# Pads, token-block sums on VectorE, an evened-out token loop and a wider slot for the query divisions in a gated attention and expert kernel

## The chip, the cores and the metric

The kernel runs on one core of one Trainium2 chip, as one launch. The metric is the device time of that launch in microseconds (us); the median of three runs of the kernel before is 2440.28 us, and they lie between 2435.78 and 2441.69 us. TensorE is called PE in the profile, its weight loads PEld, VectorE is DVE, ScalarE is ACT, GpSimd is POOL and SyncE is SP. The profile comes from one more execution of its own.

## The reference

For 2048 tokens of width 512 the result is `g*a + (1-g)*b`, all in float32:

```python
g = sigmoid((x * gate_w).sum(-1))                 # one gate per token
# a: linear attention, 32 heads of width 16
q, k, v = split(x @ wqkv);  pq, pk = phi(q), phi(k)   # phi(t) = (t+1 if t>0 else exp(t)) + 1e-6
kv = sum over tokens of pk * v;  z = sum over tokens of pk
a  = ((pq @ kv) / (pq . z + 1e-6)) @ wo
# b: 8 experts, all of them used (K = E = 8), weighted by a softmax of x @ w_gate
b  = sum over e of gates[e] * (silu(x @ w1[e]) @ w2[e])   # w1: 512x1792, w2: 1792x512
```

## The kernel before

**Numbers.** A float32 operand is split into a high part that TensorE's `float32r` form holds and the rest: ScalarE copies the high part (`act_copy`, L63), VectorE subtracts it (`split`, L267). A product then is three matmuls (`mm3`, L58 to L60: high by high, high by low, low by high).

**Seven products.** The two large products of each expert are computed on 2x2 blocks with seven block products in place of eight. So the kernel needs sums and differences of blocks of x, of the weights and of the hidden values. `prep(g, step)` makes the operands of weight group g in eight steps and writes the blocks of w2 to DRAM (`w2stash`); `x_sum` and `x_part` make those of x.

**The key stage, `keys` (L249 to L497).** It loops over 16 tiles of 128 tokens, t = 0 to 15. `load_x` brings x transposed, 512 tokens at a time; `split_x(tb, k)` splits a quarter of such a block. `g_proj(t, g)` computes keys and gate logits of a tile in two groups of columns (256 and 266); `g_done` applies phi: two ScalarE passes and one VectorE pass per group, then a high copy on ScalarE and a low pass on VectorE into the tile `pkh`, and a POOL DMA that adds the tile's keys to the key sum `pks` (L395). `load_xt` brings x untransposed and `split_xt(t)` splits it into the tile `xt`. `y_acc(t)` then adds x^T pk of the tile to four PSUM banks, 12 matmuls; it is called one tile late. Each engine takes its instructions in the order in which the program lists them, so a ScalarE copy that waits holds all that ScalarE has behind it.

Beside the tiles, at hand-set values of t, stand `x_sum` (four sums of blocks of 1024 columns for each half of the tokens; ScalarE negates the target and a POOL DMA adds the other block to it), `x_part` (splits a sum; for the second half of the tokens two SP DMAs of 512 KB store it in `xstash`), `x_keep` (stores three blocks that were split as they are) and, from t = 12, two steps of `prep(0, .)` per tile.

**The expert stage, `experts` (L501 on).** It steps through ticks u = 0, 1, 2, ... Seven ticks make a weight group. A tick's `up` does one of the seven products of the hidden layer (6 matmuls, banks a, b, c); from u = 44 on each tick also does a slice of the second product (`tick`, 6 matmuls into p, weights from the tiles `w2`). `high` and `low_h` split the hidden values into `ho`, `differ` forms their sums. Between ticks of the start stand `state` (kv of the attention, 16 float32 matmuls, u = 1), `fold` (u = 3 to 6), `gates` (u = 5), `normaliser` (u = 8), `gate_rows` (u = 10), the opening of the pool of the w2 tiles (u = 12) and `load_wb` (u = 14). Query columns pass the same way as a ninth expert, whose phi is stored to DRAM by SP (L553, 16 DMAs of 256 KB); just then `x_next` loads the second half's blocks of x back from `xstash`, on SP too.

**The divisions.** After that, in the ticks of the first four experts of the second half, `queries_first` and `queries_last` divide 512 tokens' queries by their normaliser, in slots s = 0 to 11 of 98 ticks each: s = 0 to 3 form the denominator, s = 4 to 6 invert it in four VectorE reciprocals (L860), multiply and split it, and the matmuls n (L879) spread it over the columns in slots s = 7 to 10, each followed by a VectorE multiply (L867) one slot later. The matmuls n share the two buffers of bank a with the up products.

Of the kernel before, what the change touches and what calls it, by code (L numbers as in the profile page):

```python
# [10 lines left out]
F32 = mybir.dt.float32  # L11
F32R = mybir.dt.float32r
# [25 lines left out]
def f32(ap):  # L38
    return ap.bitcast(F32)
# [3 lines left out]
def gated_mix_kernel(ctx: ExitStack, tc: tile.TileContext, xT, x, wk, wv, wqkv_q, wo, wm, out):  # L43
# [73 lines left out]
    misc = ExitStack()  # L117
    m.misc = misc.enter_context(tc.tile_pool(name="misc", bufs=1, side="right"))
    weights(m)
    keys(m)  # L120
# [128 lines left out]
def keys(m):  # L249
# [87 lines left out]
    def load_xt(tb):  # L337
        r = m.raw_tile(f"xr{tb}") if tb < 3 else room(f"xr{tb}")
        xr[tb] = r.rearrange("p (t d) -> p t d", d=D)
        nc.sync.dma_start(xr[tb], m.x[tb * TB:(tb + 1) * TB, :].rearrange("(t p) d -> p t d", p=P))  # L340
# [72 lines left out]
    def x_sum(p, step):  # L413
        a, b = raw[2 * p], raw[2 * p + 1]
        b11, b21, b12, b22 = a[:, :2], a[:, 2:], b[:, :2], b[:, 2:]
        dst, src = ((b11, b12), (b12, b22), (b22, b11), (b21, b22))[step]
        if step < 3:
            act_copy(dst, dst, scale=-1.0)
        nc.gpsimd.dma_start(dst, src, accum_op=ALU.add)

    def x_part(p, i):
# [8 lines left out]
        if i == 3:  # L430
            act_copy(h, r, scale=-1.0)
            v.scalar_tensor_tensor(lo, r, -1.0, f32(h), op0=ALU.mult, op1=ALU.subtract)
        else:
            split(r, h, lo)
        if p:
# [21 lines left out]
    ys = [dn_bank(f"y{i}") for i in range(KT)]  # L457
    x_sum(0, 0)
    for t in range(NTT - 1):
        y_acc(t)  # L460
        split_x(1, t)
    split_x(1, KT - 1)
    for t in range(NTT, NT):
        tb, tt = divmod(t, NTT)
        if t in (4, 8, 11):
            load_xt((t + 1) // 4)
        if t in (4, 5):
            load_x(t - 2)
        if t in (11, 12):
            m.load(t - 11)  # L470
        for g in range(2):
            g_proj(t, g)
        split_xt(t)
        if tb == 1:
            split_x(2, tt)
        if t in (8, 9):
            split_x(3, 2 * t - 16), split_x(3, 2 * t - 15)
        y_acc(t - 1)
        for p, at in ((0, t), (1, t - 6)):
            if at in (4, 6, 7):  # L480
                x_sum(p, at // 2 - 1 if at < 7 else 3)
            if at in (4, 6, 8, 9):
                x_part(p, {4: 1, 6: 5, 8: 3, 9: 6}[at])
        if t == 8:
            x_sum(1, 0)
        if t == 11:
            x_keep(0, (2, 0)), x_keep(2, (2, 1)), x_keep(4, (3, 1))
        if t > 11:
            m.prep(0, 2 * t - 24), m.prep(0, 2 * t - 23)
    y_acc(NT - 1)  # L490
# [10 lines left out]
def experts(m, misc):  # L501
# [42 lines left out]
    def hidden(g, f, t, dst, src):  # L544
        part, q = groups[g]
        if part.e < E:
            nc.scalar.activation(dst, src, AF.Silu)  # L547
            raw[g, f, t] = dst
            return
        if dst is src:  # L550
            dst = r_tile(f"e{g}_{f}{t}")
        phi(dst, src)
        nc.sync.dma_start(m.pqd[part.h, t, 2 * q + f], dst)  # L553

# [289 lines left out]
    def queries_first(i, s):  # L844
# [4 lines left out]
        elif s == 4:  # L849
# [6 lines left out]
            nc.gpsimd.memset(f32(Q.un[2 * NH:, 0]), 0.0)  # L856
        if s in (4, 5, 6):
            for at in ((0,), (1, 2), (3,))[s - 4]:
                r = Q.r[:, at * P:(at + 1) * P]
                v.reciprocal(r, r)  # L860
        if s == 6:
            v.tensor_mul(Q.r, Q.r, Q.gate)
            act_copy(Q.un[:NH, 0], Q.r)
            v.tensor_sub(Q.un[NH:2 * NH, 0], Q.r, f32(Q.un[:NH, 0]))
        if 8 <= s < 8 + KT:
            d = Q.d[:, s - 8]
            v.scalar_tensor_tensor(d, d, EPS, Q.ps, op0=ALU.add, op1=ALU.mult)  # L867
            nc.sync.dma_start(m.pqd[h, j, s - 8], d)

    def queries_last(i, s):  # L870
        if 0 <= s < KT:
            if s == 0:
                Q.ps = ps_tile(f"dn{i}", "a")
            for j in range(2):
                nc.tensor.matmul(Q.ps[:2 * NH, :], Q.z[:, s], Q.un[:, j], start=(s == 0 and j == 0),
                                 stop=(s == KT - 1 and j == 1))
        elif 7 <= s < 7 + KT:
            Q.ps = ps_tile(f"n{i}_{s}", "a")
            nc.tensor.matmul(Q.ps, Q.spread[:, s - 7], Q.un[:, 0], start=True, stop=True)  # L879

# [39 lines left out]
    for u in range(LAG1 + NTICK):  # L920
# [5 lines left out]
        s -= 3  # L926
        query = u >= U1 and 0 <= i < 4 and s < 12

# [128 lines left out]
```

## Time and profile before

| what | value |
|---|---|
| median of three runs | 2440.28 us |
| time of the profiled execution | 2439.3 us |
| its span | 2437.3 us |
| granted TensorE clock, mean | 0.993 |
| PE busy | 2386.7 us, 98% |
| PEld busy | 1940.2 us, 80% |
| DVE busy | 1821.5 us, 75% |
| ACT busy | 1419.3 us, 58% |
| DMA bytes | 516.52 MB |

The table's busy times are sums over stages with different limits. Matmuls overlap, so their mean duration is longer than the distance from one to the next. A row of a timeline gives start, duration, engine, line, operation, tiles and count, and in square brackets how long the engine sat idle before it and what ended that. A row of waits reads: who, on whom, us in total, times, longest. A row of a table by stretches gives the stretch, its length, then the busy time and the count of each engine, the granted clock, the DMA engines' busy share and GB/s.

### The profile page before, as it was taken

To read this page: it belongs to the slowest core of one execution; us is meant where nothing else is said; L and a number is where in the kernel's file an instruction comes from. 1 tells how busy PE (TensorE), PEld (TensorE's weight loads), DVE (VectorE), ACT (ScalarE), POOL (GpSimd) and SP (SyncE) were. 2 spreads that over 40 slices of the span, in tenths; PEclk is the share of its full clock that TensorE was granted. 3 is DMA by queue.
4 is the path that set the end of the run, shared out by engine and by line. 5 is a ranking of instruction groups with operands and counts; after the bars stand their busy time and mean duration, and the time that the engine had idled before them with its cause. 6 is when DMAs were issued, how large, how long until landed. Compare 5 with 4: busy or idle time off the path is not lost. (4 is left out here: it accounts for less than half of the span.)

```text
span 2437.3 us, 31414 instructions
## 1 busy us (share of the span) xinstructions
PE 2386.7 (98%) x10483; PEld 1940.2 (80%) x10483; DVE 1821.5 (75%) x3099; ACT 1419.3 (58%) x2656; POOL 150.6 (6%) x208
## 2 busy tenths in 40 slices
PE   8899999999999999999999999999999999999998
PEld 7777888888888888888778787878878888888876
DVE  5578878888888888888776767777676666666678
ACT  5566666666666666566655555555555555555454
POOL 2110000000000000000000000000000000000021
PEclk9999999999999999999999999999999999999999
DMA  7988888988888888988864444454544444454477
GB/s 203 252 279 287 254 280 248 271 257 265 263 260 279 251 269 253 283 256 261 284 229 117 148 138 165 140 161 148 159 156 139 138 139 146 140 145 138 135 268 271
DMA packets 298706, 516.52 MB, mean 212 GB/s; under 512 B 24352, under 2 KB 192176, under 8 KB 298160
## 3 DMA queue, kind: packets, MB, share of 16 engines
q1 hardware_dynamic: 275840, 468.03, 57.4%
q0 software_dynamic: 22704, 46.49, 10.2%
q8 instruction: 82, 1.34, 0.2%
q14 instruction: 80, 0.66, 0.1%
HBM read 344.61 MB, written 161.42 MB: 208 GB/s over the span
## 5 line engine op out<-in xcount | busy, mean ns | idle before, releaser
L58 PE MATMUL p<-ho,w 128*128 128x512 f32 x1624 | 645.6, 398 | 2.7 <-ACT p L63 1.9
L60 PE MATMUL p<-ho,w 128*128 128x512 f32 x1624 | 645.3, 397 | 0.0
L59 PE MATMUL p<-ho,w 128*128 128x512 f32 x1624 | 638.9, 393 | 0.0
L671 DVE TENSOR_TENSOR ho<-s,ho 128x512 fp32r<-128x512 f32 x784 | 536.1, 685 | 55.2 <-ACT ho L63 53.5
L63 ACT ACTIVATE ho<-s 128x512 fp32r<-128x512 f32 x784 | 486.4, 621 | 18.8 <-PE p L60 11.7
L58 PEld LDWEIGHTS p<-ho,w 128*128 128x128 f32 x1624 | 305.1, 188 | 76.1 <-ACT p L63 6.6
L60 PEld LDWEIGHTS p<-ho,w 128*128 128x128 f32 x1624 | 304.9, 188 | 74.3
L59 PEld LDWEIGHTS p<-ho,w 128*128 128x128 f32 x1624 | 305.5, 188 | 71.6
L547 ACT ACTIVATE s<-s 128x512 f32<-128x512 f32 x224 | 141.8, 633 | 280.5 <-DVE s L609 200.2
L609 DVE TENSOR_TENSOR s<-c,s 128x512 f32<-128x512 f32 x116 | 80.2, 692 | 160.3 <-PE c L60 150.7
L63 ACT ACTIVATE o<-rm 128x512 fp32r<-128x512 f32 x240 | 136.7, 570 | 82.2 <-PE a L60 63.1
L63 ACT ACTIVATE o<-rs 128x512 fp32r<-128x512 f32 x224 | 127.3, 568 | 63.7 <-PE a L60 60.1
L63 ACT ACTIVATE ws<-rm 128x512 fp32r<-128x512 f32 (+1 forms) x217 | 121.8, 571 | 59.2 <-DMA w2stash<-ws 52.5
L615 DVE TENSOR_TENSOR s<-a,s 128x512 f32<-128x512 f32 x116 | 79.9, 689 | 80.0 <-PE a L60 79.9
L547 ACT ACTIVATE s<-b 128x512 f32<-128x512 f32 x112 | 67.3, 601 | 114.2 <-PE b L60 108.9
L63 ACT ACTIVATE s<-a 128x512 f32<-128x512 f32 x116 | 69.4, 598 | 103.9 <-PE a L60 103.9
L183 DVE TENSOR_TENSOR o<-rs,o 128x512 fp32r<-128x512 f32 x168 | 114.8, 683 | 13.8 <-ACT o L63 13.0
L183 DVE TENSOR_TENSOR o<-rm,o 128x512 fp32r<-128x512 f32 x180 | 123.1, 684 | 1.5 <-ACT o L63 1.4
L201 DVE TENSOR_TENSOR ws<-rm,ws 128x512 fp32r<-128x512 f32 x164 | 112.3, 684 | 4.8 <-ACT ws L63 4.8
L63 ACT ACTIVATE s<-c 128x512 f32<-128x512 f32 x116 | 69.0, 595 | 33.4 <-PE c L60 33.3
L63 ACT ACTIVATE b<-a 128x512 f32<-128x512 f32 x116 | 67.1, 578 | 25.0 <-PE a L60 24.9
L705 POOL DMA_DIRECT2D acct<-c x28 | 23.9, 855 | 931.6 <-DVE c L701 702.2
(289 smaller groups left out, 4534.1 us busy)
## 6 DMA issues: line engine op xcount, KB each, us to landing
w<-w2stash SPq DMA_DIRECT2D x406, 512.0 KB, 3.9
w2stash<-ws SPq DMA_DIRECT2D x381, 256.0 KB, 4.3
rm<-wm SPq DMA_DIRECT2D x224, 256.0 KB, 5.3
rs<-wm SPq DMA_DIRECT2D x112, 256.0 KB, 3.7
wb<-wgtd SPq DMA_DIRECT2D x16, 512.0 KB, 5.1
acct<-c POOLq DMA_DIRECT2D x28, 256.0 KB, 6.3
acct<-d POOLq DMA_DIRECT2D x28, 256.0 KB, 5.4
acct<-k POOLq DMA_DIRECT2D x28, 256.0 KB, 5.7
```

The lines of the kernel that those rows point to most:

```text
L58: nc.tensor.matmul(ps, wh, xh, start=start, stop=False, skip_group_check=True)
L59: nc.tensor.matmul(ps, wh, xl, start=False, stop=False, skip_group_check=True)
L60: nc.tensor.matmul(ps, wlo, xh, start=False, stop=stop, skip_group_check=True)
L63: nc.scalar.activation(dst, src, AF.Copy, scale=scale, bias=bias)
L183: v.tensor_sub(two(o, 1), src, f32(two(o, 0)))
L201: v.tensor_sub(two(w, 1), src, f32(two(w, 0)))
L547: nc.scalar.activation(dst, src, AF.Silu)
L609: v.tensor_add(sn[g, 2], bank[g, "c"], sn[g, 2])
L615: v.tensor_add(sn[g, 3], bank[g, "a"], sn[g, 3])
L671: v.tensor_sub(h[:, 1], s, f32(h[:, 0]))
L705: nc.gpsimd.dma_start(m.acct[part.h, j, dt], s, accum_op=ALU.add)
```

## The change

It has five parts.

1. **Pads.** A tile of 96 bytes a partition is allotted first in the pool `misc` and first in the pool of the w2 tiles, and set to zero by GpSimd. `gat` and `mx` get 128 bytes instead of 64, and the projection weights g1 get 8576 bytes instead of 8512, so all that the pool `att` holds behind them lies 64 bytes higher.
2. **Sums on VectorE.** `x_sum` becomes one VectorE subtraction of 1024 columns; the ScalarE negations and the accumulating POOL DMAs go. The sign of one block changes with it, so `x_part` loses its special case.
3. **The token loop.** A table `beside` sets the work of each tile: two or four pieces a tile from t = 4 to 13, all of `prep(0, .)` at t = 14 and 15. `split_xt` of rows 14 and 15 moves to tiles 12 and 13. Loads move ahead, except the two weight loads, which move from t = 11, 12 to t = 12, 14; the three `x_keep` pairs move from t = 11 to t = 6, 9 and 10.
4. **The start of the expert stage.** `state` and what follows it come four to six ticks later.
5. **Queries.** Slots go from 12 to 20: one reciprocal a slot from s = 5 to 8, multiply at 9, split at 10, the matmuls n at 14 to 17. The 16 stores of the queries go from the SP queue to the POOL queue.

```diff
@@ gated_mix_kernel
+    def pad(pool):
+        nc.gpsimd.memset(pool.tile([P, 24], F32, name="pad", tag="pad", bufs=1), 0.0)
+    m.pad = pad
+    pad(m.misc)
@@ keys
-    m.gat = misc.tile([P, NT], F32, name="gat")
-    m.mx = misc.tile([P, NT], F32, name="mx")
+    m.gat = misc.tile([P, 2 * NT], F32, name="gat")[:, :NT]
+    m.mx = misc.tile([P, 2 * NT], F32, name="mx")[:, :NT]
...
-    gw = [att.tile([P, 2 * KT * G[i]], F32R, name=f"g{i}").rearrange("p (c k f) -> p c k f", c=2, k=KT) for i in range(2)]
+    gw = [att.tile([P, 2048 + 96 * i], F32R, name=f"g{i}")[:, :2 * KT * G[i]] for i in range(2)]
...
-        r = m.raw_tile(f"xr{tb}") if tb < 3 else room(f"xr{tb}")
+        xr[tb] = m.raw_tile(f"xr{tb}").rearrange("p (t d) -> p t d", d=D)
@@ x_sum
-        dst, src = ((b11, b12), (b12, b22), (b22, b11), (b21, b22))[step]
-        if step < 3:
-            act_copy(dst, dst, scale=-1.0)
-        nc.gpsimd.dma_start(dst, src, accum_op=ALU.add)
+        dst, x, y = ((b11, b12, b11), (b12, b22, b12), (b22, b22, b11), (b21, b21, b22))[step]
+        v.tensor_sub(dst, x, y)
@@ the loop over tiles
-    x_sum(0, 0)
+    load_xt(1)
+    load_x(2)
     for t in range(NTT - 1):
         y_acc(t)
         split_x(1, t)
     split_x(1, KT - 1)
+    beside = {t: [] for t in range(NTT, NT)}
+    for k in range(KT):
+        beside[4 + k // 2].append(lambda k=k: split_x(2, k))
+        beside[8 + k // 2].append(lambda k=k: split_x(3, k))
+        beside[(4, 5, 6, 6)[k]].append(lambda k=k: x_sum(0, k))
+        beside[(7, 7, 8, 9)[k]].append(lambda k=k: x_part(0, (1, 5, 3, 6)[k]))
+        beside[(10, 10, 12, 12)[k]].append(lambda k=k: x_sum(1, k))
+        beside[(11, 11, 13, 13)[k]].append(lambda k=k: x_part(1, (1, 5, 3, 6)[k]))
+        beside[14].append(lambda k=k: m.prep(0, k))
+        beside[15].append(lambda k=k: m.prep(0, 4 + k))
+    rows_of = {12: (12, 13), 13: (14, 15), 14: (), 15: ()}
     for t in range(NTT, NT):
-        if t in (4, 8, 11):
-            load_xt((t + 1) // 4)
-        if t in (4, 5):
-            load_x(t - 2)
-        if t in (11, 12):
-            m.load(t - 11)
+        if t in (4, 8):
+            load_xt(t // 4 + 1)
+        if t == 5:
+            load_x(3)
+        if t in (12, 14):
+            m.load(t // 2 - 6)
         for g in range(2):
             g_proj(t, g)
-        split_xt(t)
-        if tb == 1:
-            split_x(2, tt)
-        if t in (8, 9):
-            split_x(3, 2 * t - 16), split_x(3, 2 * t - 15)
+        for row in rows_of.get(t, (t,)):
+            split_xt(row)
         y_acc(t - 1)
-        for p, at in ((0, t), (1, t - 6)):
-            if at in (4, 6, 7):
-                x_sum(p, at // 2 - 1 if at < 7 else 3)
-            if at in (4, 6, 8, 9):
-                x_part(p, {4: 1, 6: 5, 8: 3, 9: 6}[at])
-        if t == 8:
-            x_sum(1, 0)
-        if t == 11:
-            x_keep(0, (2, 0)), x_keep(2, (2, 1)), x_keep(4, (3, 1))
-        if t > 11:
-            m.prep(0, 2 * t - 24), m.prep(0, 2 * t - 23)
+        for do in beside[t]:
+            do()
+        if t in (6, 9, 10):
+            i, key = {6: (0, (2, 0)), 9: (2, (2, 1)), 10: (4, (3, 1))}[t]
+            x_keep(i, key)
@@ hidden
-        nc.sync.dma_start(m.pqd[part.h, t, 2 * q + f], dst)
+        nc.gpsimd.dma_start(m.pqd[part.h, t, 2 * q + f], dst)
@@ queries_first
-        if s in (4, 5, 6):
-            for at in ((0,), (1, 2), (3,))[s - 4]:
-                r = Q.r[:, at * P:(at + 1) * P]
-                v.reciprocal(r, r)
-        if s == 6:
+        if 5 <= s < 9:
+            r = Q.r[:, (s - 5) * P:(s - 4) * P]
+            v.reciprocal(r, r)
+        elif s == 9:
             v.tensor_mul(Q.r, Q.r, Q.gate)
+        elif s == 10:
             act_copy(Q.un[:NH, 0], Q.r)
             v.tensor_sub(Q.un[NH:2 * NH, 0], Q.r, f32(Q.un[:NH, 0]))
-        if 8 <= s < 8 + KT:
+        if 15 <= s < 15 + KT:
@@ queries_last
-        elif 7 <= s < 7 + KT:
+        elif 14 <= s < 14 + KT:
@@ the loop over ticks
-        query = u >= U1 and 0 <= i < 4 and s < 12
+        query = u >= U1 and 0 <= i < 4 and s < 20
...
-        if u == 1:
+        if u == 5:
             state()
-        if u in (3, 4, 5, 6):
-            fold(u - 3)
-        if u == 5:
+        if u in (7, 8, 9, 10):
+            fold(u - 7)
+        if u == 11:
             gates()
-        if u == 8:
+        if u == 13:
             normaliser()
-        if u == 10:
+        if u == 15:
             gate_rows()
-        if u == 12:
+        if u == 17:
             misc.close()
             m.w2p = ctx.enter_context(tc.tile_pool(name="w2p", bufs=1, side="right", reuse_waits="tile"))
-        if u == 14:
+            m.pad(m.w2p)
+        if u == 20:
             load_wb(0)
```

More of the change, by code (lines that the diff above doesn't have):

```diff
@@ L314, in split_x @@
         split(raw[tb][:, k, :], xk(0, tb, k), xk(1, tb, k))
-    gw = [att.tile([P, 2 * KT * G[i]], F32R, name=f"g{i}").rearrange("p (c k f) -> p c k f", c=2, k=KT) for i in range(2)]
+    gw = [att.tile([P, 2048 + 96 * i], F32R, name=f"g{i}")[:, :2 * KT * G[i]] for i in range(2)]
+    gw = [g.rearrange("p (c k f) -> p c k f", c=2, k=KT) for g in gw]
     g0, g1 = gw
@@ L337, in load_xt @@
     def load_xt(tb):
-        r = m.raw_tile(f"xr{tb}") if tb < 3 else room(f"xr{tb}")
-        xr[tb] = r.rearrange("p (t d) -> p t d", d=D)
+        xr[tb] = m.raw_tile(f"xr{tb}").rearrange("p (t d) -> p t d", d=D)
         nc.sync.dma_start(xr[tb], m.x[tb * TB:(tb + 1) * TB, :].rearrange("(t p) d -> p t d", p=P))
@@ L428, in x_part @@
             h, lo = both[:, 0], both[:, 1]
[L430 to L434, printed above, removed]
+        split(r, h, lo)
         if p:
@@ L856, in queries_first @@
             nc.gpsimd.memset(f32(Q.un[2 * NH:, 0]), 0.0)
-        if s in (4, 5, 6):
-            for at in ((0,), (1, 2), (3,))[s - 4]:
-                r = Q.r[:, at * P:(at + 1) * P]
-                v.reciprocal(r, r)
-        if s == 6:
+        if 5 <= s < 9:
+            r = Q.r[:, (s - 5) * P:(s - 4) * P]
+            v.reciprocal(r, r)
+        elif s == 9:
             v.tensor_mul(Q.r, Q.r, Q.gate)
+        elif s == 10:
             act_copy(Q.un[:NH, 0], Q.r)
             v.tensor_sub(Q.un[NH:2 * NH, 0], Q.r, f32(Q.un[:NH, 0]))
-        if 8 <= s < 8 + KT:
-            d = Q.d[:, s - 8]
+        if 15 <= s < 15 + KT:
+            d = Q.d[:, s - 15]
             v.scalar_tensor_tensor(d, d, EPS, Q.ps, op0=ALU.add, op1=ALU.mult)
-            nc.sync.dma_start(m.pqd[h, j, s - 8], d)
+            nc.sync.dma_start(m.pqd[h, j, s - 15], d)
     def queries_last(i, s):
@@ L876, in queries_last @@
                                  stop=(s == KT - 1 and j == 1))
-        elif 7 <= s < 7 + KT:
+        elif 14 <= s < 14 + KT:
             Q.ps = ps_tile(f"n{i}_{s}", "a")
-            nc.tensor.matmul(Q.ps, Q.spread[:, s - 7], Q.un[:, 0], start=True, stop=True)
+            nc.tensor.matmul(Q.ps, Q.spread[:, s - 14], Q.un[:, 0], start=True, stop=True)
     def load_query(h, i):
```

1 line of the change is left out of this document (removed).

## The prediction

> **What bounds the kernel now.** I read the page first, then the busy times by stretch, then PE's waits, then the rows around each wait.
>
> ```profile
> span 2437.3 us, 31414 instructions
> PE 2386.7 (98%) x10483; PEld 1940.2 (80%) x10483; DVE 1821.5 (75%) x3099; ACT 1419.3 (58%) x2656; POOL 150.6 (6%) x208
> ```
>
> ```profile
> 30.80:123.80 93.00, 77.36 (x445) 68.12 (x444) 48.65 (x91) 50.62 (x104) 20.55 (x25) 0.91 0.83 215
> 123.80:149.00 25.20, 19.47 (x85) 14.84 (x83) 10.83 (x24) 12.46 (x22) 0.00 (x0) 0.93 0.70 228
> 149.00:190.00 41.00, 41.00 (x186) 33.98 (x187) 38.91 (x67) 33.13 (x67) 8.45 (x17) 1.00 0.98 317
> 205.00:1170.00 965.00, 965.00 (x4187) 785.77 (x4186) 805.42 (x1332) 611.89 (x1154) 40.98 (x48) 1.00 0.86 265
> ```
>
> PE is the bound: from 205 to 1170 us it never pauses, and the change leaves its matmuls as they are. It can gain only where PE stands still or runs at a lower clock, some 50 us in all (2437.3 less 2386.7). The token tiles 4 to 15 (30.8 to 123.8 us) are the worst place: 77.4 busy of 93, with a clock of 0.91, while no other engine is over 51 of 93. So the tiles there wait in turn for something, and these rows say for what:
>
> ```profile
> PE y L58 <- ACT xt L63: 15.6, 3, 6.4
> PE kv L777 <- DMA wv<-wv: 3.9, 2, 2.9
> PE a L58 <- DVE s L615: 2.1, 2, 1.8
> ```
>
> ```profile
> ACT xt L63 <- DMA xstash<-x20h: 8.5, 1, 8.5
> ACT x L63 <- DMA x<-x: 7.2, 1, 7.2
> ACT t L63 <- DMA xstash<-t: 4.5, 1, 4.5
> ```
>
> Three times y waits for the ScalarE copy of xt, 15.6 us together. Each time ScalarE itself stood before a DMA: behind tile 4 before the accumulating POOL DMA of a sum, at tile 12 before the store of x20 that frees the xt tile of row 12, behind tile 14 before the store of a split sum.
>
> **Part 1, the token tiles.** The start of the pkh copy dates each tile; the last row is PE's touch after the last y:
>
> ```profile
> 35.05 0.63 ACT L63 ACTIVATE pkh<-pk 128x512 fp32r<-128x512 f32 x1 [0.49 <-DVE pk L74]
> 57.76 0.63 ACT L63 ACTIVATE pkh<-pk 128x512 fp32r<-128x512 f32 x1 [0.49 <-DVE pk L74]
> 85.98 0.63 ACT L63 ACTIVATE pkh<-pk 128x512 fp32r<-128x512 f32 x1 [0.49 <-DVE pk L74]
> 117.30 0.63 ACT L63 ACTIVATE pkh<-pk 128x512 fp32r<-128x512 f32 x1 [0.49 <-DVE pk L74]
> ...
> 118.51 0.80 PE L58 MATMUL y<-pkh,xt 128*128 128x512 f32 x1 [6.37 <-ACT xt L63]
> 123.82 0.54 PE L559 MATMUL b<-x00h,o 128*128 128x512 f32 x1
> ```
>
> Tiles 7 to 12 (57.76 to 85.98) ran undisturbed: 28.2 us for five, 5.64 each, PE never idle. Tiles 4 to 15 took 82.25 us for eleven; at 5.64 they take 62.0, so 20.2 us go if all three waits go. The last y took 5.3 us (118.51 to 123.82) at the lowered clock after its wait; y is half of a tile's columns (12 matmuls of 512 against 24 of 256 or 266), 2.8 of the 5.64: another 2.5.
>
> Do they go? The DMA accumulation is replaced by VectorE, which needs no copy before it. The x20 store is issued at tile 6, six tiles ahead of its use, the other two pairs at 9 and 10. The store of a split sum now has two tiles (11 us) instead of less. The price of a tile on VectorE, with these durations:
>
> ```profile
> L74 DVE SCALAR_TENSOR_TENSOR pk<-pk,g 128x256 f32<-128x256 f32 x24 | 9.8, 419 | 10.5 <-ACT g L73 10.5
> L80 DVE SCALAR_TENSOR_TENSOR pkh<-pk,pkh 128x512 fp32r<-128x512 f32 x12 | 8.3, 693 | 8.4 <-ACT pkh L63 8.4
> L267 DVE TENSOR_TENSOR xt<-xr,xt 128x512 fp32r<-128x512 f32 x12 | 8.2, 684 | 8.4 <-ACT xt L63 8.4
> L267 DVE TENSOR_TENSOR t<-x,t 128x1024 fp32r<-128x1024 f32 x3 | 3.7, 1229 | 2.3 <-ACT t L63 2.3
> L391 DVE COPY lg<-g 128x10 f32<-128x10 f32 x12 | 1.9, 162 | 0.0
> L63 ACT ACTIVATE x<-x 128x1024 f32<-128x1024 f32 x5 | 5.2, 1046 | 7.2 <-DMA x<-x 7.2
> ```
>
> Base: 2 x 0.42 + 0.69 + 0.16 + 0.68 = 2.37, and 0.70 of wait for the pkh copy (8.4 over 12) = 3.07. A sum of 1024 columns, not shown before, I price at the split of the same size, 1.23 (bounds: 0, if it fits an idle spot, and 1.23). Tiles 4, 5, 8, 9: two splits and one such pass, 3.07 + 1.37 + 1.23 = 5.67. Tiles 6, 7, 10, 11: two such passes, 5.53. Tiles 12, 13 have a second xt: 6.2. Tiles 14, 15 without xt, with four steps of prep each (three to six passes of 0.68, some of half width): about 6.0 and 6.5. Over 5.64 that is 4 x 0.03 + 2 x 0.57 + 0.36 + 0.9 = 2.5; I charge 3 (bounds 0 and 14, second rival). ScalarE loses six passes of 1.05 and stays under VectorE. Eight accumulations leave the POOL queue, so the key sums behind them come sooner. The earlier loads stand on SP before anything that waits: `load_xt(2)` and `(3)` need rows already split. The weight loads come later, behind the stores of tiles 11 and 13 on SP; what needs the first is prep two tiles (11 us) on. **Sum: 20.2 + 2.5 - 3 = -19.7, I take -20** (range 0 to -23).
>
> **Part 2, the start of the expert stage.** PE waits 3.9 us for wv because kv stands one tick after the drain; four ticks later the up products cover the load. With the 2.1 us for VectorE's s and the clock of 0.93 over 25.2 us (half clock for 3.5 us, 1.7 us of work), up to 7.7 us can go. But prep of group 0, its seven stores of w2 blocks, two pairs of xstash stores, the load of group 1, wv, wo and the load of group 2 now fall into some 25 us, and 149 to 190 us shows what full DMA engines move: 317 GB/s at a share of 0.98. I take -3, nearer the full cover of wv alone (bounds -7.7 and +8, first rival). `fold`, `gates`, `normaliser`, `gate_rows` (17 POOL DMAs), the w2 pool and `load_wb` move by five ticks, and the first w2 load is due only at u = 39, so I cost them at nothing; were that cover gone, p would wait for w2 by the same five ticks.
>
> **Part 3, the divisions.** All 16 matmuls n, and the reciprocals:
>
> ```profile
> L879 PE MATMUL n<-az 128*128 128x512 f32 x16 | 7.0, 439 | 6.6 <-DVE pq L867 3.7 <-DVE az L864 2.9
> ...
> L860 DVE RECIPROCAL r<-r 32x128 f32<-32x128 f32 x16 | 14.5, 922 | 0.1
> ```
>
> PE loses 6.6 us: 2.9 because the split of the inverse comes as n is due, 3.7 because the second n waits for the bank, whose reader on VectorE is behind after four reciprocals (3.7 us). With the split at s = 10 and n at 14, the first goes; at s = 15 the backlog is long worked off, though two `differ` passes a tick stand there instead of one. **-6** (bounds -6.6 and +2, four such waits of half a microsecond).
>
> **Part 4, the query stores on POOL.** They wait for phi, and on SP they hold the loads of x behind them:
>
> ```profile
> PE c L58 <- DMA n4h<-xstash: 2.6, 1, 2.6
> ...
> SPq L553 <- DVE e L74: 9.2, 4, 3.3
> ```
>
> ```profile
> 1210.00:1220.00 10.00, 9.35 (x41) 7.25 (x39) 8.29 (x16) 6.85 (x14) 1.71 (x2) 1.00 1.05 377
> ```
>
> But the DMA engines are full then (share 1.05), so an earlier issue mostly lengthens the queue. POOL has nothing urgent: its accumulations wait for VectorE anyway. I take 0 (bounds -3 and +1).
>
> **Part 5, the pads.** What matters is which tiles move. The pool on the right ends at a fixed place, and in the built program its tiles ascend from its base in the order of allotment: the pad lies below the w2 tiles, which keep their addresses (217056, 221152 and 225248, 32 past a multiple of 64). Only `att` shifts, to multiples of 128. So p's weights stay where they are; the two small memsets are nothing. I take 0 (bounds -1 and +1, 384 g and 192 y matmuls at a few ns).
>
> **Sum against the profiled execution: 2439.3 - 20 - 3 - 6 = 2410 us.** That execution stands 1 us below the median. What cannot be told from no change is 0.3%, 7 us.
>
> **Rivals.**
>
> *The saving is met by full DMA engines (20%).* Between tile 13's end and tick 6 about 11 MB (from the tiles' shapes) want to pass in 27 us, that is 407 GB/s; at the 317 above they take 34.7, 7.7 more. The copy into a w2 store tile then waits on ScalarE, and PE behind it: 2410 + 3 + 7.7 = 2421. For it speaks the share of 0.98; against, that eight accumulations of 512 KB are gone.
>
> *VectorE paces the tiles (15%).* If, besides the pkh wait, each tile keeps the waits for ScalarE's phi (10.5 us over 24 in the row above, 0.9 a tile), VectorE needs 6.4 to 7.4 a tile, and 12 tiles cost 11 more: 2421. For it speaks that every sum of a tile already reaches 5.5; against, that such waits are short where VectorE comes late anyway.
>
> *The pads do line up the w2 tiles (3%).* The rows of p against the first product of a:
>
> ```profile
> L58 PE MATMUL p<-ho,w 128*128 128x512 f32 x1624 | 645.6, 398 | 2.7 <-ACT p L63 1.9 <-DVE d L736 0.5
> L60 PE MATMUL p<-ho,w 128*128 128x512 f32 x1624 | 645.3, 397 | 0.0
> L59 PE MATMUL p<-ho,w 128*128 128x512 f32 x1624 | 638.9, 393 | 0.0
> ...
> L58 PE MATMUL a<-x00h,o 128*128 128x512 f32 x116 | 45.7, 394 | 0.0
> L60 PE MATMUL a<-x00h,o 128*128 128x512 f32 x116 | 45.2, 390 | 0.0
> L59 PE MATMUL a<-x00l,o 128*128 128x512 f32 x116 | 45.1, 389 | 0.0
> ```
>
> p's mean is 396, a's 391: 5 ns, times 4872 is 24 us, so 2386. I hold against it the addresses above.
>
> *Slower: the key sums pace the tiles (9%).* Each tile's POOL DMA adds to the same `pks`, so each waits for the one before, and the key tiles have four buffers: tile 15 cannot write its keys before tile 11's sum has landed.
>
> ```profile
> L395 POOL DMA_DIRECT2D pks<-pk x15: 852/857/904, 26.1 to 118.1; - x15
> ...
> DMA to landing us min/median/max: 3.2/3.9/9.8
> ```
>
> From about 20 us, twelve times (0.86 + 3.9) end at 77 us, ahead of tile 15 at 97 (35 + 62). At landings of 5.6 it begins to delay; at 8.0 tile 15 comes at 126, which eats all 29 us; at 9.8, the longest seen, at 148, and the time is about 2461. For it: tiles come faster, and SP's loads are ahead of it. Against: the POOL queue loses the eight other accumulations.
>
> *VectorE holds up POOL's issues (3%).* The same chain stretches if each issue must wait for VectorE's passes: with one pass of 1.23 it ends at 20 + 12 x (0.86 + 1.23 + 3.9) = 92, still ahead of 97, with two at 107, 10 late: 2420. Against it stands the row above: the issues took 852 to 904 ns beside a VectorE that was busy 48.65 of 93 us. The Trainium skill, page "SBUF — State Buffer", section "SBUF: two separate sides", has the rule that speaks against this change: a VectorE pass can lock GpSimd out of the port through which it writes a POOL DMA's descriptors, so that a DMA of 620 ns takes 3100. By an estimate from that figure the chain would end at 104 us and the time be 2417; the trace does not agree for the passes of this stage.
>
> **How the numbers follow.** Forecast 46%, full DMA engines 20%, VectorE as the pace 15%, POOL held up 3%, lined-up w2 3%, key sums (slower) 9%, and 4% that gains and losses cancel. All but the last two are faster by over 0.3%: faster 0.87, same 0.04, slower 0.09. The range reaches from all bounds on the good side (2439.3 - 23 - 7.7 - 6.6 - 3 = 2399) to 2434, where both middle rivals come together (2410 + 11 + 11, and 2 for the rest).
>
> **What would show it.** Right: tiles 5.6 to 5.9 us apart and no y wait over 1 us; kv without a wait for wv; the idle before n near 0; the p rows unchanged at 398, 397, 393. Wrong: waits of y for pkh or of ScalarE for a w2 store, a granted clock under 0.95 in the first 150 us, or the waits on `pks` grown past 5.6 us a tile.

## The result, and the profile after

| | before | after |
|---|---|---|
| median of the runs | 2440.99 us (2435.78 to 2445.00, 4 runs) | 2406.93 us (2404.66 to 2408.38, 4 runs) |
| time and span of the profiled execution | 2439.3, 2437.3 us | 2408.4, 2406.5 us |
| granted TensorE clock, mean | 0.993 | 0.997 |

The ratio is 0.9861, with a 95% interval of 0.984 to 0.9881: faster by 1.4%. The forecast was 2410 us. The head of the page of the changed kernel:

```profile
span 2406.5 us, 31379 instructions
PE 2378.6 (99%) x10483; PEld 1936.1 (80%) x10483; DVE 1829.2 (76%) x3107; ACT 1414.8 (59%) x2650; POOL 151.8 (6%) x218
```

PE has the same 10483 matmuls. Its time outside work falls from 50.6 us (2437.3 less 2386.7) to 27.9, and its busy time by 8.1, since less of it runs at half clock. Where that lies is read by stretches (same columns as before: stretch, length, busy and count of PE, PEld, DVE, ACT, POOL, clock, DMA share, GB/s):

```profile
30.80:102.00 71.20, 71.20 (x441) 64.27 (x440) 54.11 (x93) 43.74 (x94) 11.76 (x16) 1.00 0.77 219
102.00:130.00 28.00, 24.15 (x114) 18.39 (x113) 18.45 (x32) 19.99 (x38) 0.15 (x1) 1.00 0.99 314
170.00:190.00 20.00, 17.53 (x63) 13.81 (x64) 16.77 (x28) 15.21 (x29) 0.00 (x0) 0.83 0.89 282
183.00:1148.00 965.00, 965.00 (x4187) 785.77 (x4186) 804.93 (x1330) 612.55 (x1154) 40.98 (x48) 1.00 0.86 264
```

The token tiles now fill PE without a pause (71.20 of 71.20). The start of the expert stage (102 to 130 and around 170 us) still has holes, with the DMA engines at a share of 0.99 at first. The long stretch holds exactly as many matmuls in 965 us as before, 4187. The first and the last of the twelve pkh copies of tiles 4 to 15, from ScalarE's timeline, date the tiles:

```profile
33.55 0.63 ACT L63 ACTIVATE pkh<-pk 128x512 fp32r<-128x512 f32 x1 [0.49 <-DVE pk L74]
...
96.12 0.63 ACT L63 ACTIVATE pkh<-pk 128x512 fp32r<-128x512 f32 x1 [0.49 <-DVE pk L74]
```

Eleven tiles take 62.57 us, 5.69 each, where they took 82.25 before. PE's waits from 30 to 230 us no longer name y at all; what is left is the start of the expert stage:

```profile
PE c L58 <- ACT s L63: 3.1, 1, 3.1
PE b L58 <- ACT b L63: 2.2, 1, 2.2
PE a L58 <- DVE s L618: 1.6, 1, 1.6
PE kv L780 <- DMA wv<-wv: 1.6, 2, 0.8
PE a L58 <- ACT s L63: 0.7, 1, 0.7
```

And the groups of PE, which answer those of p and n before:

```profile
L58 PE MATMUL p<-ho,w 128*128 128x512 f32 x1624 | 645.7, 398 | 2.5 <-ACT p L63 1.6 <-DVE d L739 0.5
L60 PE MATMUL p<-ho,w 128*128 128x512 f32 x1624 | 645.3, 397 | 0.0
L59 PE MATMUL p<-ho,w 128*128 128x512 f32 x1624 | 638.9, 393 | 0.0
...
L882 PE MATMUL n<-az 128*128 128x512 f32 x16 | 6.3, 393 | 0.0
```

p is unchanged and n has no idle before it. The starts of five marked matmuls in both traces split the gain by stage:

| from the start of the span to | before | after | gained in this stage |
|---|---|---|---|
| the touch after the last y | 123.82 | 100.26 | 23.6 |
| the first p | 204.30 | 182.51 | -1.8 |
| the first query product (after `x_next`) | 1337.04 | 1315.14 | 0.1 |
| p number 3800 (after the query divisions) | 2023.13 | 1992.44 | 8.8 |
| the end | 2437.25 | 2406.54 | 0.0 |

These are single executions, and the first two stages differ between executions. With the old token loop the touch comes at 123.82 us before, and at 121.99 and 119.20 in two of the kernels below that leave the loop as it was; with the new loop and the sums on VectorE it comes between 100.17 and 101.08 in nine kernels. From the touch to the first p the same three take 80.2 to 81.3 us; five with the new loop and the later ticks, among them the changed kernel, take 77.9 to 82.3 (the others have the pads elsewhere or not at all, or the query stores on SP). So the first stage gains 18 to 24 us, and the -1.8 of the second can't be told from nothing.

### The profile page after: what moved, and what is told of

It is laid out like the page before. It is cut to its first block, busy times and chain, and to the rows that moved or that the text cites. A ratio compares the mean times of both kernels' runs of the same rounds, so it can differ in the third digit from the quotient of the medians.

```text
span 2406.5 us, 31379 instructions
## 1 busy us (share of the span) xinstructions
PE 2378.6 (99%) x10483; PEld 1936.1 (80%) x10483; DVE 1829.2 (76%) x3107; ACT 1414.8 (59%) x2650; POOL 151.8 (6%) x218
## 5 line engine op out<-in xcount | busy, mean ns | idle before, releaser
L612 DVE TENSOR_TENSOR s<-c,s 128x512 f32<-128x512 f32 x116 | 80.2, 691 | 151.5 <-PE c L60 147.2
```

What stands on the lines that cost most here:

```text
L612: v.tensor_add(sn[g, 2], bank[g, "c"], sn[g, 2])
```

## Experiments

Each time is a median beside the kernel before on the same chip, which had medians from 2439.2 to 2441.1 us; single stages are read from the one profiled execution of each kernel.

### One part alone

**The token loop alone**: the kernel before with the sums on VectorE and the new table beside the tiles, nothing else.

```diff
-        dst, src = ((b11, b12), (b12, b22), (b22, b11), (b21, b22))[step]
-        if step < 3:
-            act_copy(dst, dst, scale=-1.0)
-        nc.gpsimd.dma_start(dst, src, accum_op=ALU.add)
+        dst, x, y = ((b11, b12, b11), (b12, b22, b12), (b22, b22, b11), (b21, b21, b22))[step]
+        v.tensor_sub(dst, x, y)
... (and x_part, load_xt and the loop over tiles as in the change)
```

> The kernel before with the new token loop and the sums on VectorE alone; pads, expert start, query slots and queues as before. If the three DMA waits of the tile copies were the loss, PE's touch after the last y comes at about 100 us instead of 123.8, the rest runs as before, and the time is 2440 - 20 to 24, about 2417. If the pads or the later expert start carry part of it, the touch comes at 105 us or later and the time stays above 2425.

Measured: 2419.79 us, ratio 0.9927 (0.9912 to 0.9942). The touch comes at 101.03, 22.8 earlier than before, but the first p only 16.8 earlier (187.47). The wait of PE for wv, 3.9 us before, has grown:

```profile
PE kv L772 <- DMA wv<-wv: 9.1, 1, 9.1
```

So the tiles' gain is as large as forecast, and 6.0 us of it are lost again at once (86.4 us from the touch to the first p): PE arrives earlier, the weights do not.

**The query slots alone**: the kernel before with the 20 slots of the divisions, the prediction's part 3.

```diff
-        if s in (4, 5, 6):
-            for at in ((0,), (1, 2), (3,))[s - 4]:
+        if 5 <= s < 9:
...
-        query = u >= U1 and 0 <= i < 4 and s < 12
+        query = u >= U1 and 0 <= i < 4 and s < 20
```

> The kernel before with the 20 query slots alone. Theory A, a wait costs what the trace shows as idle time of PE: the query stage (from the first dn to the end) is 6.6 us shorter. Theory B, a wait costs about 0.25 us more than its idle time since the pipe of matmuls starts anew after it: 8.8 us shorter, as between the two kernels. Everything up to the first dn stays where it was, within 0.5 us.

Measured: 2429.03 us, ratio 0.9958 (0.9942 to 0.9974), 10.9 us faster in the medians. From the first query product to the end this profile is 8.9 us shorter than before, nearly as the changed kernel is (8.8). That is theory B; the prediction had 6, and 6.6 as the bound. The last sentence of the expectation did not hold: the first query product comes 5.4 us earlier though no edit stands ahead of it, and 4.6 of that lie in the key stage, whose waits differ between executions of one kernel. Two tables by stretches, the queries before and after, confirm the 6.6 as idle time:

```profile
1336.00:1900.00 564.00, 557.03 (x2405) 448.86 (x2404) 405.25 (x700) 304.73 (x563) 22.53 (x28) 1.00 0.48 150
```

```profile
1310.00:1870.00 560.00, 559.58 (x2426) 453.45 (x2426) 408.71 (x709) 308.88 (x572) 22.51 (x28) 1.00 0.50 153
```

Idle falls from 6.97 to 0.42 us. The missing two come out of the timeline of before around two of the matmuls n:

```profile
1358.38 0.39 PE L59 MATMUL p<-ho,w 128*128 128x512 f32 x1
1358.61 0.40 PE L60 MATMUL p<-ho,w 128*128 128x512 f32 x1
1359.73 0.47 PE L879 MATMUL n<-az 128*128 128x512 f32 x1 [0.72 <-DVE az L864]
1360.04 0.39 PE L58 MATMUL b<-n2h,o 128*128 128x512 f32 x1
...
1362.59 0.40 PE L60 MATMUL p<-ho,w 128*128 128x512 f32 x1
1363.90 0.50 PE L879 MATMUL n<-az 128*128 128x512 f32 x1 [0.91 <-DVE pq L867]
1364.23 0.40 PE L58 MATMUL a<-n3h,o 128*128 128x512 f32 x1
```

Undisturbed starts are 0.23 apart; here, around the first n, they are 1.12 and 0.31 apart, so 0.97 is lost, and the bracket of its row says 0.72. It counts from the modelled end of the matmul before, 0.40 after its start, at which an undisturbed successor would have run for 0.17 already; and the matmul behind the late one comes late too. The second n loses 1.18 by the same count (its row says 0.91). Both come once in each of the four rounds of 512 queries, and four times 2.15 is 8.6, close to the 8.8.

**The pads alone taken out** of the changed kernel.

```diff
-    pad(m.misc)
-    m.gat = misc.tile([P, 2 * NT], F32, name="gat")[:, :NT]
+    m.gat = misc.tile([P, NT], F32, name="gat")
...
-            m.pad(m.w2p)
```

> The changed kernel without its pads (gat, mx and g1 at their old sizes too). My theory, the pads do nothing since the w2 tiles keep their addresses: 2407 us within 3 us, matmuls p at 398, 397 and 393 ns. Rival, the shift of the key stage's tiles by 64 bytes counts: the touch after the last y comes 1 us or more later than at 100.3 us.

Measured: 2406.46 us (2404.02 to 2407.97), against 2406.93 with them. The matmuls p stand at 397, 397 and 393 ns, and the touch comes at 100.28. The pads, where they stand, do nothing that can be measured in the time.

### A pad that moves the w2 tiles

The same 96 bytes, but in a pool of its own opened ahead of all others on the right, so that what follows lies 96 bytes lower: the w2 tiles at 216960, 221056 and 225152, multiples of 128, in place of 96 past one.

```diff
+    top = ctx.enter_context(tc.tile_pool(name="top", bufs=1, side="right"))
+    nc.gpsimd.memset(top.tile([P, 24], F32, name="top"), 0.0)
     misc = ExitStack()
...
-    pad(m.misc)
...
-            m.pad(m.w2p)
```

> The changed kernel with one pad of 96 bytes in a pool of its own above all others on the right, opened first, and the two inner pads gone, so that the w2 tiles lie 96 bytes lower, at multiples of 128. If the address of the weights is why p's matmuls are slower than the up products, p's start to start falls from about 233.5 to about 227 to 229 ns, 4872 matmuls gain 20 to 32 us, and the time is 2375 to 2387. If p is slower for another reason (its banks, its moving tiles), the time stays at 2407 within 3 us.

Measured: **2371.54 us (2368.9 to 2373.2), ratio 0.9727 (0.9712 to 0.9741)**: 35.4 us below the changed kernel, more than the 20 to 32 us expected. The groups of p, and the long stretch:

```profile
L58 PE MATMUL p<-ho,w 128*128 128x512 f32 x1624 | 634.9, 391 | 3.0 <-ACT p L63 2.2 <-DVE d L740 0.6
L59 PE MATMUL p<-ho,w 128*128 128x512 f32 x1624 | 632.4, 389 | 0.0
L60 PE MATMUL p<-ho,w 128*128 128x512 f32 x1624 | 632.2, 389 | 0.0
```

```profile
183.00:1148.00 965.00, 965.00 (x4259) 799.07 (x4258) 817.62 (x1353) 623.42 (x1175) 42.14 (x50) 1.00 0.87 268
```

In 965 us stand 4259 matmuls in place of 4187: 226.6 ns from start to start in place of 230.5, with PE at full clock and never idle in both. The page's mean durations show 7, 8 and 4 ns less for p; they understate the sum, because from start to start p falls by 6.8 ns (from 233.5 to 226.7, means over the long stretch) and the hidden products between the p groups speed up as well (in the trace of the changed kernel their starts are 226.6 to 231 ns apart, p's 231 to 238; in this one all are 226 or 227).

**The same pad in the kernel before**, with nothing else changed.

> The kernel before with nothing else than the 96-byte pool at the right end: w2 tiles at multiples of 128, old token loop, old start of the expert stage, old query slots. If the address of the weights acts by itself, p's rows fall from 398/393/397 to 391/389/389 and the time by the same 35.4 us that lie between the changed kernel and pad_on_top, to about 2405 (ratio 0.9855, within 0.0015). If the gain there came only with the other parts (less contention for the weights' reads), it is clearly less, above 2412.

Measured: 2403.72 us (2402.35 to 2405.75), ratio 0.9855 (0.984 to 0.9869), 35.5 us below before. Its long stretch:

```profile
205.00:1170.00 965.00, 965.00 (x4259) 799.33 (x4258) 816.66 (x1351) 624.00 (x1175) 40.96 (x48) 1.00 0.87 268
```

Two lines of code are worth as much as the whole change, and the two add up.

**The pad at 32 bytes**: w2 tiles at multiples of 64 that are 64 past a multiple of 128. Against the first kernel of this section:

```diff
-    nc.gpsimd.memset(top.tile([P, 24], F32, name="top"), 0.0)
+    nc.gpsimd.memset(top.tile([P, 8], F32, name="top"), 0.0)
```

> The changed kernel with the inner pads left out and 32 bytes (instead of 96, as in pad_on_top) in the pool of their own at the right end: the w2 tiles then begin at 217024, 221120 and 225216, multiples of 64 and 64 past a multiple of 128. If a multiple of 64 is enough for the weights of p, the time is that of pad_on_top, 2371.5 within 3 us, and the rows of p stand at 391/389/389. If it takes a multiple of 128, the time is that of the changed kernel, 2407 within 3 us, with 398/393/397; an effect that goes by the distance to the multiple lies between the two.

Measured: 2418.64 us (2 runs), slower than the changed kernel by 12, which neither expectation had.

```profile
183.00:1148.00 965.00, 965.00 (x4157) 780.41 (x4156) 801.58 (x1326) 610.03 (x1151) 40.94 (x48) 1.00 0.85 263
```

232.1 ns a matmul. Of the three places only the multiple of 128 is fast, and the loss is no simple distance to it: 96 past costs 3.9 ns a matmul, 64 past 5.6.

These pads move all tiles on the right together. That the w2 tiles are the ones that count shows within one execution. Near the end of the changed kernel every second w2 tile stands outside the pool on the right, in buffers of the tag `o` (`load_w2`), which begin at multiples of 128 in the built program. Twelve matmuls p use one w2 tile. Of these rows, each the first matmul of a tile, the first and the third have a tile that is 96 past, the second and the fourth one at a multiple:

```profile
2322.87 0.39 PE L58 MATMUL p<-ho,w 128*128 128x512 f32 x1
...
2325.67 0.39 PE L58 MATMUL p<-ho,w 128*128 128x512 f32 x1
...
2328.40 0.39 PE L58 MATMUL p<-ho,w 128*128 128x512 f32 x1
...
2331.21 0.40 PE L58 MATMUL p<-ho,w 128*128 128x512 f32 x1
```

The twelve take 2.80 us with the tile 96 past (233 ns each), 2.73 with the one at a multiple (227.5), then 2.81 again (234).

It does not hold for every matmul. The y matmuls of the key stage read their weights from `xt`, which lies 64 past a multiple of 128 without the pads in `att` and at a multiple with them. Undisturbed starts of y are 229.2 ns apart in the kernel without pads and 231.2 in the changed kernel, so nothing is gained at the multiple there. Why, and why 64 past is the worst in the long stretch, is open.

### The start of the expert stage

**The old ticks**: the changed kernel with `state` and what follows at u = 1, 3 to 6, 5, 8, 10, 12 and 14.

```diff
-        if u == 5:
+        if u == 1:
             state()
-        if u in (7, 8, 9, 10):
-            fold(u - 7)
+        if u in (3, 4, 5, 6):
+            fold(u - 3)
...
```

> The changed kernel with the start of the expert stage at its old ticks (state at u = 1 and so on). Tokens alone brought the touch 22.8 us forward and the first p 16.8 us; the changed kernel 23.6 and 21.8. If the later start is what kept the difference, the first p comes here at about 187 us, 4 to 5 us later than 182.5, with a wait of PE for wv of 3 us or more. If it is not, it stays at 182.5 within 1 us.

Measured: 2411.83 us, ratio 0.9875 (0.9846 to 0.9904), 4.9 slower than the changed kernel; the first p comes 5.2 later, at 187.75. The wait of kv:

```profile
PE kv L780 <- DMA wv<-wv: 7.0, 2, 6.8
```

The later ticks do take most of the wait for wv away (7.0 us here, 1.6 in the changed kernel). But what they win is only about what the earlier arrival of PE costs there.

**Two MB less.** The changed kernel without the stores of the split sums 3 and 6 of the second half; blocks 1 and 5 are read in their place (this leaves work out, as its expectation says).

```diff
-        if p:
+        if p and i in (1, 5):
             for c, t in enumerate((h, lo)):
                 nc.sync.dma_start(m.xstash[i, c], ...)
... (and the load reads blocks 1 and 5 for 3 and 6)
```

> The changed kernel without the stores of the split sums 3 and 6 of the second half's tokens (4 DMAs of 512 KB at tile 13; blocks 1 and 5 are read in their place, so the second half of the tokens comes out wrong). If full DMA engines hold the start of the expert stage, these 2 MB bring the first p matmul up to 6.7 us earlier (2 MB at 314 GB/s): it comes at about 176 us, from 182.5, and ScalarE's waits for w2stash between 90 and 190 us fall from 11 us to under 6. If VectorE's load holds it (34.7 of 40 us busy), the first p stays at 182 us within 1 us.

Measured: 2400.83 us (2400.43 to 2401.22, 2 runs), ratio 0.983 (0.9801 to 0.9858), 6.1 below the changed kernel, whose lowest run is 2404.66. The first p comes at 176.34, 6.2 earlier than there and 2.6 earlier than in the earliest of the five executions named below the table of stages (178.97 to 182.51). PE's waits from 90 to 230 us, all of them, and the stretch that had a clock of 0.83 in the changed kernel:

```profile
PE c L58 <- ACT s L63: 2.9, 1, 2.9
PE a L58 <- DVE s L618: 1.9, 2, 1.6
PE a L58 <- ACT s L63: 0.7, 1, 0.7
```

```profile
170.00:190.00 20.00, 19.51 (x84) 15.66 (x85) 17.32 (x30) 15.09 (x30) 0.00 (x0) 1.00 0.88 288
```

The wait of b for ScalarE is gone, which those five executions all have (1.6 to 3.7 us), and the half clock behind the wait for c. ScalarE's waits for w2stash between 90 and 190 us fall from 10.9 to 8.3 us, not under 6 as expected. 2.1 MB at the 314 GB/s of the row 102 to 130 above are 6.7 us, the upper end of what the first p gains. So the bytes hold this stage up; that they account for the whole delay is not shown.

**More buffers for the stores**: three of the four w2 store tiles of group 0 in free buffers of the key stage.

```diff
+    m.spare = lambda name: room(name, F32R)[:, :2 * D].rearrange("p (c f) -> p c f", c=2)
     for t in range(NTT, NT):
```

> The changed kernel with three of the four w2 store tiles of weight group 0 put into buffers of the key stage that are free by then, so that ScalarE does not wait for a store to land at tile 15. If two store tiles are too few, the 4.3 us wait of ScalarE before a w2 store tile and the 2.2 us wait of PE for bank b at 103 us go, and the first p comes 2 to 4 us earlier. If only the rate of the DMA engines counts, the wait moves a few ticks on and the first p stays at 182 us within 1 us.

Measured: 2408.04 us (2 runs), no gain; the first p comes at 184.18. The waits of PE and of ScalarE:

```profile
PE b L58 <- ACT b L63: 5.0, 1, 5.0
```

```profile
ACT yT L63 <- DMA w2stash<-wx: 6.2, 1, 6.2
```

The stores now hold the tiles yT, which share those buffers, and PE waits 5.0 for b in place of 2.2. The wait moved; the bytes stayed.

**Sooner**: pad_on_top with the work beside the tiles put one or two tiles earlier, so that the stores of the sums and the weight loads start earlier.

```diff
...
-        beside[(10, 10, 12, 12)[k]].append(lambda k=k: x_sum(1, k))
-        beside[(11, 11, 13, 13)[k]].append(lambda k=k: x_part(1, (1, 5, 3, 6)[k]))
-        beside[14].append(lambda k=k: m.prep(0, k))
-        beside[15].append(lambda k=k: m.prep(0, 4 + k))
+        beside[(9, 9, 11, 11)[k]].append(lambda k=k: x_sum(1, k))
+        beside[(10, 10, 12, 12)[k]].append(lambda k=k: x_part(1, (1, 5, 3, 6)[k]))
+    for k, t in enumerate((13, 13, 14, 14, 14, 15, 15, 15)):
+        beside[t].append(lambda k=k: m.prep(0, k))
...
-        if t in (12, 14):
+        if t in (11, 14):
...
```

> The kernel pad_on_top with the work beside the token tiles put earlier: x sums of row 0 beside tiles 4 and 5, its other halves beside 6 and 7, split of row 2 one step a tile beside 4 to 7, of row 3 beside 8, the sums of row 1 beside 9 and 11, its halves beside 10 and 12, prep of group 0 over 13 to 15, the loads of group 0 and 1 after tiles 11 and 14, the stores of x parts at 6, 8 and 9. If the bytes of the start of the expert stage are what holds it up, they begin to flow one tile (5.7 us) sooner and the first p comes 3 to 5 us earlier than in pad_on_top (181.4), the time is about 2367 (ratio to before 0.9710). Rival: the sum of bytes behind the last token tile stays as it is, or tiles with more VectorE work run over 5.7 us, and what is won is lost again: 2371 to 2374.

Measured: 2370.92 us (2369.12 to 2371.32), which can't be told from pad_on_top's 2371.54. Its waits of PE:

```profile
PE g L383 <- ACT x21h L63: 1.1, 1, 1.1
PE g L383 <- DVE x21l L275: 1.0, 1, 1.0
```

The last y ends 3.4 us later (touch at 104.17 against 100.81), since the tiles now wait for a split of x that comes just in time; the first p is 1.5 earlier (179.84), less than executions differ, and not the 3 to 5 expected. The rival held: what is won at the start is paid in the tiles.

### Sums by DMA again

The changed kernel with its new table, but the sums by a ScalarE negation and an accumulating POOL DMA as before.

```diff
-        v.tensor_sub(dst, x, y)
+        if step < 3:
+            act_copy(dst, dst, scale=-1.0)
+        nc.gpsimd.dma_start(dst, src, accum_op=ALU.add)
... (and x_part with its special case)
```

> The changed kernel with the sums of x as before, by ScalarE negation and accumulating POOL DMA, in the new table of tiles. If even spacing and earlier loads alone free the tiles, the touch stays at 100 to 102 us. If the accumulation in the path of ScalarE is itself the cost, ScalarE waits 5 to 7 us at each of the four tiles where a sum follows another (t = 5, 6, 10, 12), the touch comes at 108 us or later, and the time is 2413 us or more.

Measured: 2426.49 us, ratio 0.9935 (0.9913 to 0.9958), 19.6 above the changed kernel. The touch comes at 123.31, where it was before the change (123.82). ScalarE's waits for DMAs of the sums and PE's waits of y, up to 125 us:

```profile
ACT x L63 <- DMA x<-x: 18.1, 3, 10.2
...
ACT t L63 <- DMA x<-x: 5.5, 2, 4.4
```

```profile
PE y L58 <- ACT xt L63: 9.2, 2, 6.5
PE y L58 <- ACT pkh L63: 6.7, 3, 5.3
```

The new table alone gains nothing here. It does take away two of ScalarE's three waits of before, those for the stores of x20h (8.5 us) and of t (4.5): in this kernel ScalarE waits for no store to xstash up to 125 us. But in the new table the sums by DMA hold ScalarE for 23.6 us in five waits, up to 10.2, in place of one of 7.2, with the tile's own copies queued behind it. So with this table the whole gain at the touch hangs on the sums. What sums on VectorE are worth in the old loop, where two of the three waits are for stores, was not run. From the touch to the first p this kernel takes 76.5 us against 80.5 before, with the tiles as late as before; the later ticks can be the reason, but its stores and weight loads are timed differently too.

### The query stores back on SP

```diff
-        nc.gpsimd.dma_start(m.pqd[part.h, t, 2 * q + f], dst)
+        nc.sync.dma_start(m.pqd[part.h, t, 2 * q + f], dst)
```

> The changed kernel with the stores of the queries issued by SP again instead of POOL. The prediction costed the move at 0 (bounds -3 and +1): the stretch up to the use of x_next (1202 us here) and the end then stay within 1 us of the changed kernel, 2407, with a wait for n4h of 2.5 to 3.5 us before c in both. Rival: the move is worth what the prediction's far bound said, then this kernel loses up to 3 us, 2410, and the wait grows by as much.

Measured: 2404.52 us (2403.84 to 2405.21, 2 runs), 2.4 below the changed kernel's median and at the edge of its range. The wait that the prediction spoke of, in this kernel and in the changed one:

```profile
PE c L58 <- DMA n4h<-xstash: 2.5, 1, 2.5
```

```profile
PE c L58 <- DMA n4h<-xstash: 3.0, 1, 3.0
```

The move to POOL shortens nothing. Whether it costs a microsecond or two can't be told: the stretch from p number 2000 to 2300, around this place, takes 146.7 us in the changed kernel, 144.1 in this one, and between 144.3 and 146.2 in five others that keep the stores on POOL.

## Why the prediction was right, and where it was not

The time was 2408.4 us in the profiled execution against 2410 forecast. That close a fit is partly luck: two steps were too small and one gained nothing.

*Part 1, -20: right, -23.6.* All three y waits are gone, and the tiles stand 5.69 us apart within the 5.6 to 5.9 named. Of the 23.6, the eleven tiles give 19.7 (20.2 forecast), the way from the last pkh copy to the touch 2.4 (6.5 us before, 4.1 after; 2.5 forecast), and 1.5 stand ahead of tile 4, where the sum had nothing. The failing term is the charge of 3 us for VectorE, whose durations were added up to 5.5 to 6.5 us a tile: at 5.69 against 5.64 the eleven tiles paid 0.6. VectorE was busy 54.1 of 71.2 us, 4.3 of a tile's 5.69, and PE never waited. The size of the loss before is itself one execution's, so 18 to 24 us is what can be said. The prediction named two causes, one wait behind an accumulating DMA and two before stores, and the kernel with sums by DMA fits both: the new table takes the waits for the stores away, and the DMA sums, left in it, cost as much as all three did. How the gain divides between the two is open.

*Part 2, -3: did not come; +1.8, which can't be told from 0.* The wait for wv fell from 3.9 to 1.6 us, and the clock from 102 to 130 us was 1.00, as the step said. What it missed is that part 1 brings PE to this place some 20 us earlier while the bytes keep their time. ScalarE's waits for a w2 store tile, which the prediction named as a sign of being wrong, rose from 6.1 us in two waits (115 to 250 us before) to 11.2 in six (90 to 230 us after). The first rival had that mechanism and put it at 10.7 us (7.7 and the 3); 3 to 5 of it came. The parts can't be added here: the tiles alone lose 6.0 us in this stage, and the later ticks then win 5.2 of it back. That the bytes hold the stage up is shown by the kernel with 2 MB less, which is 6.1 us faster; the kernel with more buffers gains nothing.

*Part 3, -6: right mechanism, -8.8.* The term, 6.6 us of idle time, was mis-sized: from start to start the waits cost 8.6, beyond the bound of 6.6.

*Part 4, 0: held within what can be told.* *Part 5, 0: held*: 2406.46 without pads against 2406.93. The reading of the addresses was right, and so the rival of lined-up w2 tiles did not come true by this change. Its price was wrong: 24 us from the difference of the mean durations, 35.4 measured once the tiles were moved, since from start to start p was 6.8 ns slower and not 5, and the products beside it were slowed too.

*The other rivals.* VectorE as the pace: refuted by PE's 71.20 of 71.20. The key sums: their DMAs landed in 3.7 us in the median and 9.0 at most, in the rows for `pks` after:

```profile
L402 POOL DMA_DIRECT2D pks<-pk x15: 845/855/906, 23.3 to 100.3; - x15
...
DMA to landing us min/median/max: 3.2/3.7/9.0
```

The point from which they decide, 5.6, was not reached in the median, and single long landings were absorbed. The same row speaks on POOL's issues: 845 to 906 ns each, beside a VectorE busy for three quarters of the time. The rule of the Trainium skill, page "SBUF — State Buffer", section "SBUF: two separate sides", by which a VectorE pass can lock GpSimd out while it writes a DMA's descriptors, showed no such delay here either. That section ties the lock to VectorE's two-port modes, with a copy as its example, and says that a tensor_tensor has no such mode; the new sums and the splits are TENSOR_TENSOR, so these rows hardly test it.

## What to carry to other kernels

When a stage is sped up, ask when the bytes of the next one can be there: the gain of an earlier arrival ends where the DMA engines are full, and more buffers or earlier ticks then only move the wait. A DMA that an in-order engine waits for in the middle of a tile costs everything queued behind it: with the new table, eight VectorE passes of 1.2 us in place of eight such sums were worth some 20 us here. And look up the addresses of the weights that a long loop reads: a pad helps only if it moves them, and two lines in the right place were worth as much as the whole change. A microsecond or two of one stage is explained only when several executions agree on it.

## What the runs showed of the hardware that was not expected

- **The start address of weights can set the pace of TensorE.** With the w2 tiles at a multiple of 128 bytes, 96 past and 64 past one, a 128x512 matmul takes 226.6, 230.5 and 232.1 ns from start to start, at full clock and with PE never idle. The neighbouring products, whose operands did not move, slow down too. For the y matmuls it does not show: 229.2 ns with their weights 64 past, 231.2 at a multiple. The Trainium skill, page "SBUF — State Buffer", section "Operand start alignment", says which start addresses are legal, and that this is about legality, not speed; these runs add the speed.
- **A short pause can lower the clock.** In the first of these rows of before, PE has stood still for 2.06 us; the second, by stretches, shows it busy throughout soon after at a clock of 0.51:

```profile
20.36 0.50 PE L58 MATMUL y<-pkh,xt 128*128 128x512 f32 x1 [2.06 <-ACT pkh L63]
```

```profile
21.70:25.10 3.40, 3.40 (x10) 2.65 (x9) 2.04 (x6) 2.33 (x6) 0.00 (x0) 0.51 0.51 210
```

  In the changed kernel the wait of 3.1 us for c is followed by the 0.83 of the row 170 to 190. Half clock over 6.8 us (0.17 of 20 us, doubled) costs 3.4, as much again as the wait itself. The length of the pause does not decide alone: in the kernel with 2 MB less the wait of 2.9 us for c at the same place is followed by a clock of 1.00. The Trainium skill, page "TensorE: Matmul & The Clock Gate", section "What's actually happening", ties the drop to an idle window of about 3.4 us; in the trace of before a pause of 2.06 us was enough.
- **The idle time of a row understates a wait of PE** by about a quarter of a microsecond (0.97 against 0.72, 1.18 against 0.91), because it is counted from a modelled end.
- **VectorE's durations overlap.** In the timeline of the changed kernel the second of these passes starts 1.14 us after the first, which lasts 1.23. So a sum of durations, of which the charge of 3 us in part 1 was formed, overstates what VectorE needs, by 0.09 us at this pass.

```profile
70.92 1.23 DVE L424 TENSOR_TENSOR x<-x 128x1024 f32<-128x1024 f32 x1
72.06 0.41 DVE L74 SCALAR_TENSOR_TENSOR pk<-pk,g 128x256 f32<-128x256 f32 x1
```
